# One PSUM pool for both phases of an attention-then-experts kernel, and another order of its first microseconds

## The chip, the cores and the metric

The kernel runs on one core of a Trainium2 chip. The core has five engines with queues of their own: TensorE (PE, with its weight loads PEld), VectorE (DVE), ScalarE (ACT), GpSimd (POOL) and SyncE (SP), which here only issues DMAs. DMAs issued from POOL and SP run on 16 DMA engines that all queues share. The metric is the time of one execution on the device, in microseconds (us); the median of several runs counts.

## What is computed

The reference is a gated attention unit without softmax, followed by a mixture of experts. Cut to what matters:

```python
scores = (1.0 / S) * np.matmul(z, z.transpose(0, 2, 1))    # z: 8 x 2816 x 64
attn = np.maximum(scores, 0.0) ** 2
x = (u * np.matmul(attn, v)).reshape(B * S, D)             # u, v: 8 x 2816 x 256
...
y_dense = np.maximum(x @ w1_dense, 0.0) @ w2_dense         # 256 -> 512 -> 256
expert_idx = np.argmax(x @ w_gate, axis=1)                 # 8 experts
for e in range(E):
    mask = expert_idx == e
    h = np.maximum(x[mask] @ w1[e], 0.0)
    y_moe[mask] = gate_w[mask, None] * (h @ w2[e])         # gate_w: softmax weight of the expert
out = y_dense + y_moe
```

Inputs and output are float32; the products on TensorE are bfloat16.

## The kernel before

**Phase one, attention.** There are 8 batches of 22 blocks of 128 rows (nK = 22, 176 blocks in all). Queries are taken in groups of 2 or 4 blocks, six groups to a batch. For a group, `scores` (line 390) multiplies z's turned blocks on PE into a pair of PSUM banks, and `relu` (line 412) offers two elementwise steps for each such tile: a scaled relu out of PSUM into a float32 buffer r (`first`, lines 420 and 422), and a square of r into the bfloat16 tile A (`second`, lines 433 and 435). The relu can run on ACT or DVE; the square on ACT or DVE, or, in the first two groups, on ACT or POOL. `av` (line 577) then multiplies A by v into an o tile in two passes over the keys (line 603), for two query blocks at a time, and `gate_x` (line 626) multiplies o by u on DVE (line 630) and issues a transposing DMA. Blocks of A that an earlier group has already as their mirror image are turned by DMA (line 487) and not computed again.

All of this is put in order while the program is built: `now` is the modelled time on PE, `free` that at which ACT, DVE and POOL come free, `offer`, `best` and `run` hand elementwise steps to whichever engine ends first by the model, and `need` takes the keys in the order in which A (`key_at`) and v (`v_at`, line 527) are expected. On the chip each engine runs its own instructions strictly in that order.

PSUM has eight banks. Phase one divides them into NS = 4 pairs, tags b0 to b3 of the pool ps, handed out by `take_pair` and given back by `give_pair`.

**The start.** The first batch's z comes in four parts (keys 0 to 3, 4 to 9, 10 to 15, 16 to 21), each loaded by SP, cast and doubled to bfloat16 by `cast_z0` (parts 0 and 2 on DVE, 1 on ACT, 3 on POOL), turned on PE (line 191) and copied out of PSUM by `turn_z0` (parts 0 and 2 on DVE, 1 and 3 on ACT). `scores` calls `turn_z0` as its keys ask for it, with four keys to spare: the first call, for keys 0 to 3, turns parts 0 and 1 ahead of its own matmuls. POOL issues v in four parts with `load_v`, two early and two after the constants: a select for the triangle ntri, four iotas, the cast of part 3 and the load of the gating weights wg stand between or behind them. `gate=True` puts a one-column memset on DVE in front of a load.

**Routing.** After 11 blocks `routing` computes gate logits (`logits`, line 651, which reads wg), picks the expert and the row (`route_a`, `route_pre`, which reads ntri, `route_b`), and one `scatter` per tick (line 749, on POOL) moves a block of rows to its expert's place in DRAM. A tick is a step of one block.

**Phase two, experts.** Each `slot` (line 1025) takes 256 rows of one expert: a transposed `fetch` on SP (line 924), the dense first layer and the expert's first layer (`up`, line 964: eight matmuls into an h_ps tile of two banks, line 973, and a relu on ACT, line 976), and two halves of 128 rows (`half`, line 991: `down` puts dense and expert result into one yy tile of one bank, line 982; ACT copies the dense part, line 999; DVE multiplies and adds, line 1000; POOL scatters the rows to the output, line 1002). On PE ups and halves alternate. The h tiles come from a pool psS with three buffers and the yy tiles from psY with two; both are opened after the pool of phase one is closed (lines 1192 to 1194). The last two routing groups use these pools too (`small`, line 645). A last part of the program runs only if the rows need more tiles than usual.

Of the kernel before, what the change touches and what calls it, by code (L numbers as in the profile page):

```python
# [8 lines left out]
F32 = mybir.dt.float32  # L9
# [3 lines left out]
ALU = mybir.AluOpType  # L13
AX = mybir.AxisListType
ET = mybir.EngineType
P = 128
# [3 lines left out]
def kernel(  # L20
# [12 lines left out]
    nc = tc.nc  # L33
    B, S, D = u.shape
# [43 lines left out]
    NS = 4  # L78
    attention = ExitStack()
    ps = attention.enter_context(tc.tile_pool(name="ps", bufs=1, space=bass.MemoryType.PSUM))  # L80
    late = {}
# [104 lines left out]
    def turn_z0(n):  # L186
# [19 lines left out]
        if n % 2:  # L206
            give_pair(z0_turned[n], x)

    load_v(0, 0, 4)
    cast_z0(0)  # L210
    cast_z0(1)
    load_v(0, 1, 4)
    nc.gpsimd.affine_select(out=ntri[:], in_=ntri[:], compare_op=ALU.is_ge,
                            fill=0.0, base=0, pattern=[[-1, P]],
                            channel_multiplier=1)
    ti = aw.tile([P, G, E], I32, name="ti", tag="xT", bufs=8)
# [6 lines left out]
    pj = const.tile([P, 1], I32, name="pj")  # L223
    nc.gpsimd.iota(pj[:], pattern=[[0, 1]], base=0, channel_multiplier=1)
    cast_z0(3)
    load_v(0, 2, 4, gate=False)
    load_v(0, 3, 4, gate=False)
    z0_left = list(range(len(parts0)))
    z0_cast = [0.0, 1.1, 0.0, 2.8]
    z0_turned = [0.0] * len(parts0)  # L230
    free.update(act=1.1, pool=4.2)

    nc.gpsimd.dma_start(out=wg[:], in_=moe_w_gate.rearrange("(c p) e -> p c e", p=P))
    sf = const.tile([P, N // T2], F32, name="sf")
# [4 lines left out]

    def small_constants():  # L240
        nc.vector.tensor_copy(desc8[:], ti[:])
# [148 lines left out]
    def scores(n, ks, x=None):  # L390
# [4 lines left out]
        c = w * P  # L395
        while n == 0 and z0_left and parts0[z0_left[0]][0] <= ks[-1] + 4:
            turn_z0(z0_left.pop(0))
# [11 lines left out]
        relu(n, ks, s, c, now[0] + 0.2, sx)  # L409
        run(now[0])  # L410

    def relu(n, ks, s, c, ready, sx):
# [37 lines left out]

        offer(ready, 1, {"act": (0.12 + c / 600, first), "dve": (0.1 + c / 480, first)}, half)

# [74 lines left out]
    def v_at(n, k):  # L527

        return 3.3 + 2.6 * (4 * k // nK) if n == 0 else 0.0

# [46 lines left out]
    def av(n, i, between):  # L577
# [9 lines left out]
        ox = take_pair()  # L587
        o = banks(ox, "o")
        for p in range(2):
            rest = list(range(nK))  # L590
# [54 lines left out]
    def small(q, name, shape):  # L645
        if q < nQ - 2:
            return banks(bank_of[q], name, shape)
        tag = "y" if q == nQ - 2 else "s"
        return late[tag].tile(list(shape), F32, name=name, tag=tag)

# [313 lines left out]
    def up(xT, ws):  # L964

        m = xT.shape[1]
        h_ps = late["s"].tile([P, 4, 2, P], F32, name="h_ps", tag="s")
        n = m // len(ws)
# [22 lines left out]
    def half(s, j):  # L991
# [3 lines left out]
        yd, ys = take("yd"), take("ys")  # L995
        y = late["y"].tile([P, 2, D], F32, name="yy", tag="y")
        down(y, 0, hd, lambda f: w2d[:, f, :], j)
# [191 lines left out]
    while jobs:  # L1189
        jobs.pop(0)[1]()  # L1190
        run(9e9)
    attention.close()
    late["s"] = pool("psS", 3, space=bass.MemoryType.PSUM)
    late["y"] = pool("psY", 2, space=bass.MemoryType.PSUM)
    for s in range(NT - MAYBE + 2):
# [47 lines left out]
```

## Time and profile before

| what | us |
|---|---|
| runs of the kernel before | 904.14, 905.04, 910.75 |
| median | 905.04 |
| the profiled execution | 909.34 |
| its span, first to last instruction | 907.6 |
| PE busy | 862.3 (95%) |
| ACT busy | 697.8 (77%) |
| DVE busy | 667.2 (74%) |
| POOL busy | 468.1 (52%) |
| first matmul of A with v (line 603) | starts at 10.1 |
| last one | starts at 550.1 |
| first h_ps matmul | starts at 552.0 |

The profile comes from one execution, and its span leaves out what lies before the first and after the last instruction. A row of the timeline gives the start, the length, the engine (a q behind it means its queue processor), the line and the operation, what is written from what, how many like instructions are merged in it, and in brackets how long the engine was idle before and what released it. Matmuls overlap one another in the array, so a row's mean duration is longer than the step from one to the next. The clock granted to TensorE was 0.998 over the span.

### The profile page before, as it was taken

The numbers are of one execution on the slowest core, as the hardware profiler recorded it, in microseconds if no ns is written. First come the engines' busy times: TensorE is split into PE (matmuls) and PEld (weight loads), VectorE is DVE, ScalarE is ACT, GpSimd is POOL, SyncE is SP. The second block draws the span as 40 slices with busy tenths as digits, with TensorE's granted clock in tenths as the row PEclk, the third lists the DMA queues.
The fourth block names the chain that finished last, engine by engine and source line by source line (L and its number), as shares of the span: only waits on it lengthen the run. The fifth ranks groups of instructions, "written<-read, shape, count | busy, mean of one in ns | idle before, by whom it ended". The sixth has DMA issues, their size and how long they took to land.

```text
span 907.6 us, 30096 instructions
## 1 busy us (share of the span) xinstructions
PE 862.3 (95%) x12178; PEld 754.2 (83%) x12178; DVE 667.2 (74%) x1268; ACT 697.8 (77%) x871; POOL 468.1 (52%) x510
## 2 busy tenths in 40 slices
PE   7999999999999999999999999988989898999996
PEld 5898798898898888889889877877878787888885
DVE  7998898898889889889889976456644444546554
ACT  8988798888889879879879964666666666776664
POOL 8202343343353444343334354777778777877454
PEclk9999999999999999999999999999999999999999
DMA  9999999999999999999998874645434453443332
GB/s 179 156 192 165 184 193 169 201 196 180 213 182 186 199 178 187 199 175 195 205 178 153 163 126 94 129 113 116 112 101 115 108 109 107 109 103 100 88 89 83
DMA packets 288238, 136.80 MB, mean 151 GB/s; under 512 B 258526, under 2 KB 265950, under 8 KB 287200
## 3 DMA queue, kind: packets, MB, share of 16 engines
q1 hardware_dynamic: 263552, 79.40, 52.5%
q0 software_dynamic: 24544, 55.44, 26.3%
q8 instruction: 96, 1.57, 0.7%
q14 instruction: 46, 0.38, 0.1%
HBM read 61.54 MB, written 37.03 MB: 109 GB/s over the span
## 4 chain that ended last, share of the span: by engine, by line
PE 70%; POOL 10%; issue 9%; DVE 4%; ACT 3%; DMA 2%; POOLq 0%; another core or an unknown queue 0%; DVEq 0%; SPq 0%; ACTq 0%
PE o L603 41%; PE yy L982 9%; PE h_ps L973 9%; PE s L405 9%; POOL out_dram L1002 7%; POOL zr L987 1%; DMA out_dram<-ring,ix 1%; ACT A L433 1%; ACT r L420 1%; DVE r L422 1%; PE lg L659 1%; POOL A L435 1%; DMA wall<-A 1%; DVE ring L1000 1%; ACT ring L999 1%
## 5 line engine op out<-in xcount | busy, mean ns | idle before, releaser
L603 PE MATMUL o<-vb,A 64*128 64x256 bf16 x7184 | 458.9, 269 | 3.1 <-POOL A L435 1.3
L603 PEld LDWEIGHTS <-A 64*128 64x128 bf16 x7184 | 378.8, 94 | 44.2 <-issue 3.3
L749 POOL DMA_INDIRECT xs<-pays,pi x176 | 191.9, 1090 | 283.0 <-DVE pi L747 232.1
L420 ACT ACTIVATE r<-s 128x1024 f32<-128x1024 f32 (+1 forms) x252 | 247.1, 1011 | 44.4 <-PE s L405 42.1
L976 ACT ACTIVATE ring<-h_ps 128x1024 bf16<-128x1024 f32 x180 | 184.6, 1027 | 96.1 <-PE h_ps L973 61.1
L433 ACT ACTIVATE A<-r 128x1024 bf16<-128x1024 f32 (+1 forms) x238 | 242.1, 1047 | 7.3 <-DMA wall<-A 4.6
L1000 DVE SCALAR_TENSOR_TENSOR ring<-yy,me,ring 128x256 f32<-128x256 f32 x179 | 85.6, 481 | 154.3 <-ACT ring L999 82.9
L435 DVE TENSOR_TENSOR A<-r 128x1024 bf16<-128x1024 f32 x151 | 182.9, 1221 | 4.0 <-ACT r L420 3.0
L422 DVE TENSOR_SCALAR r<-s 128x1024 f32<-128x1024 f32 (+1 forms) x145 | 175.0, 1214 | 8.7 <-PE s L405 6.0
L1002 POOL DMA_INDIRECT out_dram<-ring,me x140 | 147.1, 1051 | 66.2 <-DVE ring L1000 31.2
L982 PEld LDWEIGHTS <-ring 128*128 128x128 bf16 x1432 | 138.9, 98 | 44.6 <-issue 28.9
L405 PE MATMUL s<-zT 64*128 64x512 bf16 (+1 forms) x874 | 145.1, 355 | 1.8 <-ACT zT L199 0.6
L982 PE MATMUL yy<-w2d,ring 128*128 128x256 bf16 x716 | 107.3, 272 | 22.8 <-DVE ring L1000 20.2
L982 PE MATMUL yy<-ring 128*128 128x256 bf16 x716 | 107.6, 273 | 0.3 <-issue 0.3
L973 PE MATMUL h_ps<-ring 128*128 128x256 bf16 (+1 forms) x872 | 94.6, 254 | 1.2
L973 PE MATMUL h_ps<-ring,w1d 128*128 128x256 bf16 x720 | 93.1, 272 | 2.3 <-DVE pays L630 1.6
L999 ACT COPY ring<-yy 128x256 f32<-128x256 f32 x179 | 67.7, 378 | 29.2 <-PE yy L982 18.1
L960 DVE COPY ring<-wall 128x2048 bf16 x109 | 81.8, 765 | 10.2 <-issue 6.2
L630 DVE TENSOR_TENSOR pays<-o,ut 128x512 bf16<-128x512 f32 x88 | 60.2, 685 | 30.6 <-PE o L603 29.0
L973 PEld LDWEIGHTS <-ring 128*128 128x128 bf16 x872 | 73.0, 98 | 11.7 <-DVE ring L960 2.7
L973 PEld LDWEIGHTS <-w1d 128*128 128x128 bf16 x720 | 69.9, 98 | 11.0 <-issue 3.0
L405 PEld LDWEIGHTS <-zT 64*128 64x128 bf16 x874 | 54.2, 94 | 17.5 <-issue 6.7
(122 smaller groups left out, 426.6 us busy)
## 6 DMA issues: line engine op xcount, KB each, us to landing
ut<-in_u_dram SPq DMA_DIRECT2D x88, 256.0 KB
vb<-in_v_dram POOLq DMA_DIRECT2D x7, 1408.0 KB
wall<-in_moe_w_dram POOLq DMA_DIRECT2D x16, 256.0 KB
xs<-pays,pi POOLq DMA_INDIRECT x176
zr<-in_z_dram POOLq DMA_DIRECT2D x7, 352.0 KB
out_dram<-ring,me POOLq DMA_INDIRECT x140
ring<-xs SPq DMA_TRANSPOSE x114
xT<-pays SPq DMA_TRANSPOSE x88
```

Of the source, the lines that this page charges most:

```text
L405: nc.tensor.matmul(out=s[:, h, y * c:(y + 1) * c], lhsT=zT[r, k + h, :], rhs=zT[r, i0:i0 + w, :], start=True, stop=True)
L420: nc.scalar.activation(r[:, :, :c], s[:, :, :c], AF.Relu, scale=1.0 / S)
L422: nc.vector.tensor_scalar(out=r[:, :, :c], in0=s[:, :, :c], scalar1=1.0 / S, scalar2=0.0, op0=ALU.mult, op1=ALU.max)
L433: nc.scalar.activation(a, r, AF.Square)
L435: (nc.gpsimd if eng == "pool" else nc.vector).tensor_mul(a, r, r)
L603: nc.tensor.matmul(out=o[:, j, 0:D], lhsT=block(n, k, i + j - i0)[r], rhs=v_of[b][r, k, :], start=(p == 0 and x == 0), stop=(p == 1 and x ...
L749: ins = nc.gpsimd.indirect_dma_start(out=xs, out_offset=bass.IndirectOffsetOnAxis(ap=pi[:], axis=0), in_=pays[:, g % (2 * G), 0:ROW].bitca ...
L973: nc.tensor.matmul(out=h_ps[:, f, hs, :], lhsT=w1(c, f), rhs=xT[:, hs, c, :], start=(c == 0), stop=(c == 1))
L976: nc.scalar.activation(h[:, :, 0:m * P], h_ps[:, :, 0:m, :].rearrange("p f h t -> p f (h t)"), AF.Relu)
L982: nc.tensor.matmul(out=y[:, k, :], lhsT=h[:, f, j * P:(j + 1) * P], rhs=w2(f), start=(f == 0), stop=(f == 3))
L1000: nc.vector.scalar_tensor_tensor(out=ys, in0=y[:, 1, :], scalar=me[:, j, 0:1], in1=yd, op0=ALU.mult, op1=ALU.add)
L1002: ins = nc.gpsimd.indirect_dma_start(out=out, out_offset=bass.IndirectOffsetOnAxis(ap=ids[j], axis=0), in_=ys, in_offset=None, bounds_chec ...
```

## The change

The diff does five things. The pool ps stays open for the whole kernel: the pairs that phase one leaves become, for phase two, one pair for both yy tiles (a bank each, two views of one tile) and three pairs for h, with the pair of the last o at the end of that row; `next_h` and `next_y` take them in rotation. The first call of `scores` turns only part 0 ahead of its matmuls, and part 1 with the second call. The relu of the first score tile can only go to DVE, and the model runs 0.4 us further there, so that it is put in before the next part is turned. On POOL the iotas stand ahead of v, the four parts of v are issued in one go with a gate on the first alone, and the cast of part 3 follows; the expected times of v (`v_at`) and of POOL's start are moved to match. The load of wg and the select for ntri go into `small_constants`, which is called at tick 2.

```diff
-    attention = ExitStack()
-    ps = attention.enter_context(tc.tile_pool(name="ps", bufs=1, space=bass.MemoryType.PSUM))
+    ps = pool("ps", 1, space=bass.MemoryType.PSUM)
+    last_o = []
...
-    load_v(0, 0, 4)
-    cast_z0(0)
-    cast_z0(1)
-    load_v(0, 1, 4)
-    nc.gpsimd.affine_select(out=ntri[:], in_=ntri[:], compare_op=ALU.is_ge,
...
     nc.gpsimd.iota(pj[:], pattern=[[0, 1]], base=0, channel_multiplier=1)
+    for h in range(4):
+        load_v(0, h, 4, gate=h == 0)
+    cast_z0(0)
+    cast_z0(1)
     cast_z0(3)
-    load_v(0, 2, 4, gate=False)
-    load_v(0, 3, 4, gate=False)
...
-    z0_cast = [0.0, 1.1, 0.0, 2.8]
+    z0_cast = [0.0, 1.1, 0.0, 2.4]
...
-    free.update(act=1.1, pool=4.2)
-
-    nc.gpsimd.dma_start(out=wg[:], in_=moe_w_gate.rearrange("(c p) e -> p c e", p=P))
+    free.update(act=1.1, pool=2.4)
...
     def small_constants():
+        nc.gpsimd.dma_start(out=wg[:], in_=moe_w_gate.rearrange("(c p) e -> p c e", p=P))
+        nc.gpsimd.affine_select(out=ntri[:], in_=ntri[:], compare_op=ALU.is_ge,
...
-        while n == 0 and z0_left and parts0[z0_left[0]][0] <= ks[-1] + 4:
+        while n == 0 and z0_left and parts0[z0_left[0]][0] <= ks[-1] + (4 if ks[0] else 1):
...
-        run(now[0])
+        run(now[0] + (0.4 if n + ks[0] == 0 else 0.0))
...
+        ways = {"act": (0.12 + c / 600, first), "dve": (0.1 + c / 480, first)}
+        if n + ks[0] == 0:
+            del ways["act"]
+        offer(ready, 1, ways, half)
...
-        return 3.3 + 2.6 * (4 * k // nK) if n == 0 else 0.0
+        return 2.8 + 2.5 * (4 * k // nK) if n == 0 else 0.0
...
+        if q == nQ - 1:
+            return next_h(name, shape)
+        a, b = shape[1:]
+        return next_y()[:, 0:a * b].rearrange("p (a b) -> p a b", b=b)
+
+    def next_h(name, shape):
+        late["h"].append(late["h"].pop(0))
+        return banks(late["h"][-1], name, shape)
+
+    def next_y():
+        late["y"].append(late["y"].pop(0))
+        return late["y"][-1]
...
-        h_ps = late["s"].tile([P, 4, 2, P], F32, name="h_ps", tag="s")
+        h_ps = next_h("h_ps", (P, 4, 2, P))
...
-        y = late["y"].tile([P, 2, D], F32, name="yy", tag="y")
+        y = next_y().rearrange("p (k d) -> p k d", d=D)
...
-    attention.close()
-    late["s"] = pool("psS", 3, space=bass.MemoryType.PSUM)
-    late["y"] = pool("psY", 2, space=bass.MemoryType.PSUM)
+    other = [x for _, x in pairs if x not in last_o]
+    assert len(other) == NS - 1
+    yy = banks(other.pop(0), "yy")
+    late["y"] = [yy[:, x, :] for x in range(2)]
+    late["h"] = other + last_o
```

More of the change, by code (lines that the diff above doesn't have):

```diff
@@ L207, in turn_z0 @@
             give_pair(z0_turned[n], x)
-    load_v(0, 0, 4)
-    cast_z0(0)
-    cast_z0(1)
-    load_v(0, 1, 4)
-    nc.gpsimd.affine_select(out=ntri[:], in_=ntri[:], compare_op=ALU.is_ge,
-                            fill=0.0, base=0, pattern=[[-1, P]],
-                            channel_multiplier=1)
     ti = aw.tile([P, G, E], I32, name="ti", tag="xT", bufs=8)
@@ L240, in small_constants @@
     def small_constants():
+        nc.gpsimd.dma_start(out=wg[:], in_=moe_w_gate.rearrange("(c p) e -> p c e", p=P))
+        nc.gpsimd.affine_select(out=ntri[:], in_=ntri[:], compare_op=ALU.is_ge,
+                                fill=0.0, base=0, pattern=[[-1, P]],
+                                channel_multiplier=1)
         nc.vector.tensor_copy(desc8[:], ti[:])
@@ L449, in half @@
             offer(t + 0.15, 4, ways, done)
-        offer(ready, 1, {"act": (0.12 + c / 600, first), "dve": (0.1 + c / 480, first)}, half)
+        ways = {"act": (0.12 + c / 600, first), "dve": (0.1 + c / 480, first)}
+        if n + ks[0] == 0:
+            del ways["act"]
+        offer(ready, 1, ways, half)
     def can_turn(n, m):
@@ L588, in av @@
         o = banks(ox, "o")
+        last_o[:] = [ox]
         for p in range(2):
@@ L647, in small @@
             return banks(bank_of[q], name, shape)
-        tag = "y" if q == nQ - 2 else "s"
-        return late[tag].tile(list(shape), F32, name=name, tag=tag)
+        if q == nQ - 1:
[8 more added lines that the diff above has]
+        return late["y"][-1]
     def logits(q):
```

## The prediction

> **What bounds the kernel now.** I read the page's busy shares and its chain of waits first, then the stages, and then the two places the change touches: the first 25 us and the seam between the phases. The chain, by engine and by line:
>
> ```profile
> PE 70%; POOL 10%; issue 9%; DVE 4%; ACT 3%; DMA 2%; POOLq 0%; another core or an unknown queue 0%; DVEq 0%; SPq 0%; ACTq 0%
> PE o L603 41%; PE yy L982 9%; PE h_ps L973 9%; PE s L405 9%; POOL out_dram L1002 7%; POOL zr L987 1%; DMA out_dram<-ring,ix 1%; ACT A L433 1%; ACT r L420 1%; DVE r L422 1%; PE lg L659 1%; POOL A L435 1%; DMA wall<-A 1%; DVE ring L1000 1%; ACT ring L999 1%
> ```
>
> TensorE carries the chain. The stages say where it doesn't (stretch, its length, then busy us of PE, PEld, DVE, ACT, POOL, the clock, the DMA share and GB/s):
>
> ```profile
> core 0 of [0], span 907.6 us
> core 0: us, PE busy (x) PEld busy (x) DVE busy (x) ACT busy (x) POOL busy (x), PEclk, DMA share, GB/s
> 0.00:10.00 10.00, 6.99 (x68) 4.77 (x68) 6.64 (x12) 6.18 (x7) 7.84 (x20) 1.00 0.80 162
> 5.00:6.00 1.00, 1.00 (x14) 0.59 (x13) 0.08 (x1) 0.48 (x1) 1.00 (x5) 1.00 0.75 110
> 10.00:25.00 15.00, 12.63 (x178) 8.79 (x180) 12.39 (x16) 14.26 (x16) 12.71 (x9) 1.00 1.16 187
> 25.00:50.00 25.00, 24.45 (x400) 21.18 (x398) 24.83 (x34) 23.71 (x26) 4.28 (x8) 1.00 0.92 162
> 400.00:500.00 100.00, 99.72 (x1707) 88.22 (x1708) 88.16 (x160) 85.88 (x95) 39.39 (x39) 1.00 1.04 181
> 600.00:640.00 40.00, 35.72 (x320) 30.85 (x318) 20.96 (x41) 23.37 (x37) 31.44 (x38) 1.00 0.55 119
> 760.00:820.00 60.00, 57.56 (x526) 51.14 (x525) 28.63 (x50) 40.98 (x65) 46.39 (x54) 1.00 0.44 106
> ```
>
> From 400 to 500 us PE idles 0.28 us in 100. What can be won in the attention phase lies in the first 25 us, where PE idles 3.0 and 2.4 us. Right after that DVE and ACT are full (24.83 and 23.71 of 25), so early gains must also be gains of the elementwise engines. In the second phase PE idles 4.3 us of 40, then 2.4 of 60; no edit touches its steady pattern, only its first instant and its buffers.
>
> **The start, part by part.** GpSimd's queue in order of time (start, length):
>
> ```profile
> 3.01 1.33 POOL L130 DMA_DIRECT2D vb<-in_v_dram  x2 [1.47 <-DVE vb L129]
> 4.35 0.31 POOL L213 TENSOR_SCALAR_AFFINE_SELECT ntri<-ntri 128x128 bf16<-128x128 bf16 x1
> 4.60 0.67 POOL L218 IOTA tok<- 128x176 int32 x1
> 5.23 0.12 POOL L220 IOTA te<- 128x8 int32 x1
> 5.32 0.19 POOL L222 IOTA it<- 128x88 int32 x1
> 5.48 0.12 POOL L224 IOTA pj<- 128x1 int32 x1
> 5.56 0.81 POOL L180 CAST zn<-z 128x768 bf16<-128x768 f32 x1
> 6.33 1.07 POOL L130 DMA_DIRECT2D vb<-in_v_dram  x2
> 7.39 0.73 POOL L233 DMA_DIRECT2D wg<-in_moe_w_gate_dram  x1
> 8.12 1.93 POOL L435 TENSOR_TENSOR A<-r 128x1024 bf16<-128x1024 f32 x1
> ```
>
> The four iotas (0.67 + 0.12 + 0.19 + 0.12 = 1.10 us) move into the 1.47 us in which the queue waits for the gate of the first v load: free, with 0.37 to spare. The select and the wg load (0.31 + 0.73 = 1.04) go to tick 2, behind the first squares; the next user of both is the first routing, many ticks later, and POOL is busy 4.28 us of 25 in that stretch, which hides them; without that cover they would cost 1.04 us of POOL. The queue becomes four v issues, 3.01 + 1.33 + 1.07 = 5.41, then the cast of z's last part to 6.22. So POOL reaches its first square at about 6.2 instead of 8.12, if a score tile has been through its first relu by then. The second v load also loses its gate, a memset on DVE that is already passed: nothing.
>
> VectorE around the same time:
>
> ```profile
> 4.13 0.42 DVE L197 COPY zT<-zp 128x512 bf16<-128x512 bf16 x1 [0.69 <-PE zp L191]
> 4.47 0.60 DVE L184 CAST zn<-z 128x768 bf16<-128x768 f32 x1
> 6.29 0.56 DVE L197 COPY zT<-zp 128x768 bf16<-128x768 bf16 x1 [1.21 <-PE zp L191]
> 6.81 1.23 DVE L422 TENSOR_SCALAR r<-s 128x1024 f32<-128x1024 f32 x1
> ```
>
> The first part of z is turned by 4.55. In the new order the scores of keys 0 to 3 stand next on PE, so they are there by about 5.0, when DVE ends its cast (5.07). The relu takes 1.23; the idle time ahead of the copy at 6.29 is 1.21. It fits almost exactly, ends at 6.30 and delays that copy by 0.01. Behind it queue only that copy and DVE's next relu. What the new order delays is the turning of the second part on PE, by the four small matmuls set in front of it, 0.2 to 0.4 us, and so ACT's copy of it and the second score tile. I take 0.2, which the next steps hide, since ACT is spared its first relu (about 1 us; the row stands below).
>
> So r stands at 6.30 and POOL's first square can start at about 6.4: 1.7 us earlier. What does PE gain? Its two stalls after the first keys:
>
> ```profile
> 14.68 0.55 PE L603 MATMUL o<-vb,A 64*128 64x256 bf16 x4 [1.08 <-DMA vb<-in_v_dram]
> ```
>
> ```profile
> 22.96 0.79 PE L603 MATMUL o<-vb,A 64*128 64x256 bf16 x8 [0.85 <-POOL A L435]
> ```
>
> The first is the landing of v. The last two v parts are issued about 2.1 us earlier (6.33 to 4.3), but the DMA share is 1.16 in the stretch they land in, so the load is limited by bandwidth; what is won is the hole of 5 to 6 us (share 0.75, so 0.25) and some priority over the transposes that come after 11 us. The bounds are 0 and 2.1; I take 0.4, nearest to the hole. The second stall ends on a square of POOL, whose chain starts 1.7 earlier: all of the 0.85 can go, and the next limit is then DVE and ACT. Together 0.4 + 0.85 = 1.25. Against it the elementwise limit: the early start wins one relu on DVE and one square on POOL, which is one score tile. Their prices:
>
> ```profile
> L435 DVE TENSOR_TENSOR A<-r 128x1024 bf16<-128x1024 f32 x151 | 182.9, 1221 | 4.0 <-ACT r L420 3.0
> L422 DVE TENSOR_SCALAR r<-s 128x1024 f32<-128x1024 f32 (+1 forms) x145 | 175.0, 1214 | 8.7 <-PE s L405 6.0 <-POOL A L435 1.5 <-ACT A L433 0.6
> ```
>
> ```profile
> L420 ACT ACTIVATE r<-s 128x1024 f32<-128x1024 f32 (+1 forms) x252 | 247.1, 1011 | 44.4 <-PE s L405 42.1 <-DVE A L435 0.7 <-POOL A L435 0.6
> L433 ACT ACTIVATE A<-r 128x1024 bf16<-128x1024 f32 (+1 forms) x238 | 242.1, 1047 | 7.3 <-DMA wall<-A 4.6 <-DVE r L422 1.0 <-issue 0.4
> ```
>
> A tile costs ACT 1.01 + 1.05 = 2.06 and DVE 1.21 + 1.22 = 2.43; together they make one per 1 / (1/2.06 + 1/2.43) = 1.12 us. So one tile ahead is 1.1 us, the smaller of the two. **Start: 1.1 us won**, bounds 0 (v sets everything) and 1.9 (0.4 + 0.85 plus the rest of the 1.7).
>
> A rule speaks against part of it. The two v issues that lay beside VectorE's SBUF cast took 1.33 together, the two beside its copy out of PSUM 1.07: a difference of 0.13 each. The Trainium skill (SBUF — State Buffer, section Who interferes with whom) says that a VectorE copy or cast in its two-port mode locks GpSimd out of the shared SBUF port for the whole instruction, and that descriptor generation suffers. By that rule the new third issue, which falls on the cast of 4.47 to 5.07, could stand for up to its 0.60, and the start would win 0.5 instead of 1.1; the trace supports a tenth of a microsecond, not the full lock.
>
> **The seam.** Before, phase two has its own PSUM pools, opened when the old one closes:
>
> ```profile
> 551.98 1.03 PE L973 MATMUL h_ps<-ring,w1d 128*128 128x256 bf16 x8 [1.64 <-DVE pays L630]
> ```
>
> PE waits 1.64 us for VectorE's last gating product, though that product reads only the last o. With one pool the first h tile takes a pair that was freed earlier, so PE goes straight on. Next late is slot 1's transposed fetch:
>
> ```profile
> 550.05 1.21 SPq L924 DMA_TRANSPOSE ring<-xs  x1
> ```
>
> PE would want it after two ups and the small logits, 551.98 - 1.64 + 0.87 + 0.87 + 0.2 = 552.3 (0.87 per up is in the chain row further down; 0.2 for the small logits is an estimate). The queue's issue alone lasts to 551.26 and its landing isn't shown; before, PE used it here and didn't wait:
>
> ```profile
> 553.92 1.03 PE L973 MATMUL h_ps<-ring,w1d 128*128 128x256 bf16 x8
> ```
>
> So the landing lies between 551.26 and 553.92. I put it at 552.7, near the middle, which costs 0.4 of the 1.64. **Seam: 1.2 us won**, bounds 0.4 and 1.64; the first output scatter moves with it, so the POOL part of the later chain does too.
>
> The rest of the pool edit changes names only: three h buffers of two banks and two y buffers of one bank, taken in the same rotation.
>
> **Sum.** 1.1 + 1.2 = 2.3 us. The profiled execution took 909.34 us (span 907.6, so 1.7 outside it), 4.3 above the median of the three runs, 905.04. I predict 907.0 for the like execution and 905.04 - 2.3 = 902.7 us as the median.
>
> **Rivals.** *Seam or start gives nothing* (0.20): the fetch or v's landing takes over; then 904, with only one of the terms left. *The new plan drifts* (0.12): the order after the start is made from modelled times, so other relus land on other engines over 500 us. PE's busy time from 40 to 540 us bounds it:
>
> ```profile
> sum 500.00, PE 495.99; mean PE 19.84
> ```
>
> That is 4.0 us of idle time, so a drift is worth up to 4 us either way: 902.7 + 4.0 = 906.7, or 898.7. *More than counted* (0.06): all bounds at once, 1.9 + 1.64 plus some drift, 900 to 901.
>
> *Slower: the two y buffers become one* (0.07). They are now halves of one tile that lives through the whole phase. If waits are made per tile and not per bank, each half must wait for the readers of the half before. Rows for the price, the relu that may stand ahead on ACT, ACT's copy, DVE's product, and the up that lies between two halves on PE:
>
> ```profile
> 555.00 1.02 ACT L976 ACTIVATE ring<-h_ps 128x1024 bf16<-128x1024 f32 x1
> 555.91 0.37 ACT L999 COPY ring<-yy 128x256 f32<-128x256 f32 x1
> ```
>
> ```profile
> 556.31 0.48 DVE L1000 SCALAR_TENSOR_TENSOR ring<-yy,me,ring 128x256 f32<-128x256 f32 x1
> ```
>
> ```profile
> 570.11 0.87 PE h_ps L973 x8
> ```
>
> Copy and product with three handovers (0.04 each, an estimate) are 0.97, against 0.87 of cover: 0.1 us of stall per half, and up to 1.1 where a relu stands ahead of the copy. Times 179 halves that is 18 to 200 us; with half a relu, 0.6 x 179 = 107, about 1010 us. It decides as soon as one half waits for the other. Against it: the SBUF rings of this kernel are cut from single tiles as well, and there PE reads one slice of ring while ACT writes another without a wait (the relu at 555.00 lies beside this product):
>
> ```profile
> 555.23 0.60 PE L982 MATMUL yy<-ring 128*128 128x256 bf16 x4
> ```
> That is SBUF, so the trace doesn't settle it for PSUM. The Trainium skill (PSUM — Partial Sum Buffer, section PSUM bank collisions raise a hardware error) asks for semaphores by bank, and the halves lie in two banks; by that rule nothing waits and this rival is worth nothing.
>
> **How the numbers follow.** The forecast as worked out has 0.55; with the rivals above that is 1.00. One per cent, 9 us, is about what a measurement of this kernel can tell from no change. Only the y rival passes it on the slow side; with 0.01 for a drift that large, slower is 0.08. Faster by 9 us would need more than all idle time named here: 0.02. Within 1%: 0.90. The range reaches from the bounds with some drift, 899.5, up to the drift against the change, 906.7, and a little of the spread of runs, 907.5; it leaves out the y rival and little else.
>
> **What would show it.** The start: a POOL square beginning near 6.4, DVE's first relu near 5.1, the v stall on PE shorter or earlier, the 0.85 us stall on POOL's square gone. The seam: no wait of the first h_ps for pays, 0 to 0.4 us for a fetch instead. The y halves: the wait of yy for DVE's ring product as before; if it grows by tens of microseconds, the y rival is true. I'm wrong if PE's idle time in the middle of phase one moves by more than 2 us, or if the first output scatter doesn't come earlier.

## The result: slower by four per cent, and the profile after

| what | before | after |
|---|---|---|
| median of 6 runs each, us | 906.32 | 943.45 |
| lowest to highest | 904.14 to 911.93 | 940.36 to 946.36 |
| the profiled execution | 909.34 | 944.55 |
| its span | 907.6 | 942.8 |
| last matmul of A with v starts | 550.1 | 552.1 |
| from there to the end of the span | 357.5 | 390.7 |

The ratio of the medians is 1.040, with a 95% interval of 1.036 to 1.044. The forecast was 902.7 us, 899.5 to 907.5. In the kernel after, line numbers have moved: o is L605, h_ps L985, its relu L988, yy L994, ACT's copy of yy L1011, VectorE's product L1012 and the fetch L936.

The last two rows of the table place the loss: phase one ends 2 us later, and phase two is 33 us longer. The 2 us say little: nine traces of kernels with the phase one of the kernel before, it among them, end it between 547.7 and 552.3 us. The stages of the kernel after, with the columns of the prediction's stages:

```profile
10.00:25.00 15.00, 11.71 (x145) 7.67 (x145) 11.67 (x16) 12.40 (x15) 10.41 (x8) 0.89 1.13 205
25.00:50.00 25.00, 24.41 (x392) 20.96 (x394) 24.86 (x33) 23.57 (x25) 4.31 (x8) 1.00 0.83 131
400.00:500.00 100.00, 99.72 (x1711) 88.38 (x1709) 88.06 (x159) 86.25 (x96) 39.23 (x40) 1.00 1.00 181
600.00:640.00 40.00, 35.08 (x297) 28.75 (x296) 20.18 (x46) 25.21 (x38) 28.97 (x35) 1.00 0.41 103
760.00:820.00 60.00, 54.20 (x457) 44.37 (x456) 24.16 (x46) 39.54 (x57) 43.19 (x49) 1.00 0.40 100
```

The middle of phase one is as it was: PE is busy 99.72 of 100 us in both. From 760 to 820 us PE, DVE, ACT and POOL all do less in the same time (from 600 to 640 us all but ACT). The matmul count says it best: 457 instead of 526 from 760 to 820 us. No engine there has become the bound; everything waits. For what, PE's waits tell (what waited, for what, us in all, times, longest). After:

```profile
PE yy L994 <- DVE ring L1012: 28.6, 80, 1.3
PE yy L994 <- issue: 3.5, 19, 0.5
PE o L605 <- DMA vb<-in_v_dram: 1.9, 1, 1.9
PE h_ps L985 <- DMA ring<-xs: 1.8, 2, 1.1
```

Before:

```profile
PE yy L982 <- DVE ring L1000: 20.2, 22, 2.4
PE yy L982 <- issue: 2.3, 4, 0.9
```

The sum has grown by 8.4 us only, and whoever stops there misses the loss. The number of places went from 22 to 80, and the single wait became shorter: a few long holds have become a steady pattern. The weight loads carry more of it (busy us and mean ns, then idle time before them), since they wait beside a blocked matmul:

```profile
L994 PEld LDWEIGHTS <-ring 128*128 128x128 bf16 x1432 | 138.8, 97 | 84.8 <-issue 70.0
```

Before, this row (L982) has 44.6 us of idle time. The pattern itself stands in the timeline of the kernel after, two halves from the middle of phase two:

```profile
781.54 1.02 ACT L988 ACTIVATE ring<-h_ps 128x1024 bf16<-128x1024 f32 x1 [0.50 <-PE h_ps L985]
781.66 0.60 PE L994 MATMUL yy<-w2d,ring 128*128 128x256 bf16 x4 [0.16 <-DVE ring L1012]
781.66 0.75 PEld L994 LDWEIGHTS <-ring 128*128 128x128 bf16 x7 [0.34 <-issue]
...
782.10 0.60 PE L994 MATMUL yy<-ring 128*128 128x256 bf16 x4
...
782.53 1.04 PE L985 MATMUL h_ps<-ring,w1d 128*128 128x256 bf16 x8
...
782.73 0.37 ACT L1011 COPY ring<-yy 128x256 f32<-128x256 f32 x1 [0.17 <-PE yy L994]
...
783.14 0.48 DVE L1012 SCALAR_TENSOR_TENSOR ring<-yy,me,ring 128x256 f32<-128x256 f32 x1 [0.58 <-ACT ring L1011]
...
783.67 0.60 PE L994 MATMUL yy<-w2d,ring 128*128 128x256 bf16 x4
```

Read it as one chain; call the time from the start of one half to the start of the next a turn. The eight matmuls of a half take 781.66 to 782.70. ACT copies from 782.73, VectorE multiplies from 783.14 to 783.62, and the next half starts at 783.67, 0.05 behind the product that read the other half of the same PSUM tile. A turn takes 2.01 us: 1.04 of matmuls and 0.97 of copy, product and handovers. PE's own work in a turn is about 1.75: 0.87 for the half's eight matmuls, from the first start to the start of what follows, and as much for the up between. The rest is PE standing still, in pieces too small to look like a stall.

The mean turn over phase two comes from the first and last start of the yy rows (duration min, median, max in ns, then the two starts). Before:

```profile
L982 PE MATMUL yy<-w2d,ring x716: 269/272/273, 554.8 to 898.7; 128*128 128x256 bf16 x179
```

After:

```profile
L994 PE MATMUL yy<-w2d,ring x716: 269/271/273, 556.5 to 936.4; 128*128 128x256 bf16 x179
```

179 halves have 178 steps: 343.9 / 178 = 1.93 us before, 379.9 / 178 = 2.13 after. The difference, 0.20 us x 178 = 36 us, is the whole of the loss; the span grew by 35.2 us, since the first yy comes 1.7 later and the stretch behind the last one is 2.5 shorter.

### The profile page after: what moved, and what is told of

The parts are those of the page before. It is cut to its first block, busy times and chain, and to the rows that moved or that the text cites. A ratio compares the mean times of both kernels' runs of the same rounds, so it can differ in the third digit from the quotient of the medians.

```text
span 942.8 us, 30096 instructions
## 1 busy us (share of the span) xinstructions
PE 883.6 (94%) x12178; PEld 755.6 (80%) x12178; DVE 665.8 (71%) x1269; ACT 717.1 (76%) x871; POOL 470.2 (50%) x508
## 5 line engine op out<-in xcount | busy, mean ns | idle before, releaser
L605 PE MATMUL o<-vb,A 64*128 64x256 bf16 x7184 | 460.6, 269 | 4.2 <-DMA vb<-in_v_dram 1.9
L605 PEld LDWEIGHTS <-A 64*128 64x128 bf16 x7184 | 379.5, 94 | 46.0 <-issue 5.2
L761 POOL DMA_INDIRECT xs<-pays,pi x176 | 197.3, 1121 | 282.1 <-DVE pi L759 231.6
L988 ACT ACTIVATE ring<-h_ps 128x1024 bf16<-128x1024 f32 x180 | 183.3, 1019 | 93.5 <-PE h_ps L985 83.0
L1012 DVE SCALAR_TENSOR_TENSOR ring<-yy,me,ring 128x256 f32<-128x256 f32 x179 | 86.4, 483 | 187.6 <-ACT ring L1011 75.6
L994 PEld LDWEIGHTS <-ring 128*128 128x128 bf16 x1432 | 138.8, 97 | 84.8 <-issue 70.0
L1014 POOL DMA_INDIRECT out_dram<-ring,me x140 | 154.6, 1104 | 86.5 <-DVE ring L1012 56.8
L420 DVE TENSOR_SCALAR r<-s 128x1024 f32<-128x1024 f32 x147 | 178.0, 1218 | 10.4 <-PE s L403 9.7
L994 PE MATMUL yy<-w2d,ring 128*128 128x256 bf16 x716 | 106.9, 271 | 40.3 <-DVE ring L1012 28.6
L994 PE MATMUL yy<-ring 128*128 128x256 bf16 x716 | 107.4, 273 | 0.0
L1011 ACT COPY ring<-yy 128x256 f32<-128x256 f32 x179 | 66.6, 372 | 48.9 <-PE yy L994 29.9
L985 PE MATMUL h_ps<-ring,w1d 128*128 128x256 bf16 x720 | 92.9, 272 | 1.8 <-DMA ring<-xs 1.8
L985 PE MATMUL h_ps<-ring 128*128 128x256 bf16 (+1 forms) x872 | 93.2, 253 | 0.0
L972 DVE COPY ring<-wall 128x2048 bf16 x109 | 76.2, 714 | 17.6 <-issue 9.2
L985 PEld LDWEIGHTS <-ring 128*128 128x128 bf16 x872 | 73.9, 98 | 6.8
L985 PEld LDWEIGHTS <-w1d 128*128 128x128 bf16 x720 | 69.8, 98 | 10.2 <-DMA ring<-xs 2.0
```

The lines of the kernel that those rows point to most:

```text
L420: nc.vector.tensor_scalar(out=r[:, :, :c], in0=s[:, :, :c], scalar1=1.0 / S, scalar2=0.0, op0=ALU.mult, op1=ALU.max)
L605: nc.tensor.matmul(out=o[:, j, 0:D], lhsT=block(n, k, i + j - i0)[r], rhs=v_of[b][r, k, :], start=(p == 0 and x == 0), stop=(p == 1 and x ...
L761: ins = nc.gpsimd.indirect_dma_start(out=xs, out_offset=bass.IndirectOffsetOnAxis(ap=pi[:], axis=0), in_=pays[:, g % (2 * G), 0:ROW].bitca ...
L985: nc.tensor.matmul(out=h_ps[:, f, hs, :], lhsT=w1(c, f), rhs=xT[:, hs, c, :], start=(c == 0), stop=(c == 1))
L988: nc.scalar.activation(h[:, :, 0:m * P], h_ps[:, :, 0:m, :].rearrange("p f h t -> p f (h t)"), AF.Relu)
L994: nc.tensor.matmul(out=y[:, k, :], lhsT=h[:, f, j * P:(j + 1) * P], rhs=w2(f), start=(f == 0), stop=(f == 3))
```

## The experiments

The kernels were run in six batches, each on one chip beside runs of the kernel before. That kernel's median was 909.4, 915.4, 874.6, 917.1, 877.4 and 907.8 us in them, so ratios are taken within a batch. The first theory was the slow rival of the prediction: the two y halves have become one tile of PSUM, the memory into which PE writes its sums, and every half waits for the readers of the half before. Its own rival was that the new order of the start or the seam disturbs the later plan.

**The shared tile alone, and everything but the shared tile** (batch 1). `one_y_alone` is the kernel before with this one edit:

```diff
...
-    late["y"] = pool("psY", 2, space=bass.MemoryType.PSUM)
+    late["y"] = pool("psY", 1, space=bass.MemoryType.PSUM)
+    yy = late["y"].tile([P, 2, 4 * P], F32, name="yy")
+    late["yy"] = [yy[:, x, :] for x in range(2)]
```

> The kernel before with one edit: both yy buffers are halves of one PSUM tile that lives through phase two, a bank each, taken in rotation; pools, start and seam stay. Theory (each half of yy waits for VectorE's product of the half before, since the wait is made for the tile): the second phase takes some 33 us more, 906 + 33 = 939 us, and the yy matmuls wait for VectorE in about 80 places instead of 22. Rival (waits are made by bank, so the halves stay independent, and the 35 us come from the seam, the h rotation or the start): 906 us, within 2.

`after_two_y` is the kernel after, with pair 2 in a pool of its own that is closed at the end of phase one and makes room for two y tiles:

```diff
...
-    yy = banks(other.pop(0), "yy")
-    late["y"] = [yy[:, x, :] for x in range(2)]
+    other.remove(YP)
+    ypair.close()
+    late["y"] = pool("psY", 2, space=bass.MemoryType.PSUM)
```

> The changed kernel with one edit: the pair of banks that held the yy tile becomes a pool of its own with two yy tiles, a fresh one for each half; everything else of the change stays. Theory (the shared yy tile costs the 33 us): 943 - 33 = 910 us, the wait of yy for VectorE back to about 22 places. Rival (one pool for the h tiles, the seam or the start costs it): stays at 935 us or more.

Measured: `one_y_alone` 939.32 us, ratio 1.034 (1.029 to 1.039); `after_two_y` 908.52, ratio 1.000 (0.997 to 1.003). The waits follow. `one_y_alone`:

```profile
PE yy L988 <- DVE ring L1006: 25.6, 79, 1.4
```

`after_two_y`:

```profile
PE yy L996 <- DVE ring L1014: 18.4, 21, 1.9
```

One edit alone brings 79 places, and its removal alone goes back to 21. The cause is settled by this pair. All other parts of the change together gave nothing that could be measured; the interval of `after_two_y` reaches some 2.4 us down, so a gain as small as the forecast's 2.3 us isn't ruled out by the times alone.

**One buffer** (batch 2). Does the tile with two banks act like a single buffer? `y_one_buffer` is the kernel before with `pool("psY", 1, ...)`, the tiles taken as before.

> The kernel before with a single yy buffer (one pool buffer instead of two), nothing else. Theory (two views of one tile work as one buffer): the same second phase as with the shared tile, 939 us, the yy matmuls waiting for VectorE in about 80 places. Rival (the shared tile is more than the loss of a buffer, or less, since the halves still overlap in part): differs from 939 by more than 5 us.

Measured: 945.88 us, ratio 1.033 (1.027 to 1.039), where the shared tile had 1.034 in batch 1. Its waits:

```profile
PE yy L982 <- DVE ring L1000: 28.6, 84, 1.4
```

So the second bank of the shared tile bought nothing.

**Start alone and seam alone** (batch 1). `start_alone` has every edit of the start and no other; `seam_alone` has the one pool of the change, but with separate y tiles.

> The kernel before with the start edits alone: GpSimd's order, the scores of the first keys ahead of the turning of the next, first relu on VectorE; PSUM pools as before. Theory (TensorE reaches v's last part sooner, idles 1.9 us for it, its granted clock falls to one half for about 3.4 us, and the first phase ends 2 us later): 906 + 2 = 908 us. Rival (the predicted gain of one score tile, 1.1 us, and the 2 us of the changed kernel came from one slow landing of v): 905 us.

> The kernel before with the one PSUM pool, but with two yy tiles in a pool of their own; start as before. Theory (the first h no longer waits for VectorE's last gating product, 1.6 us, but the transposed fetches of the second and third tile then end last, so nothing of it is kept): 906 us, within 1. Rival (the predicted seam gain): 905 us or less, with the first output scatter 1.2 us earlier after the last matmul of phase one.

Measured: 908.99 us, ratio 0.9995 (0.997 to 1.002), and 906.88, ratio 0.998 (0.996 to 1.001). Neither gives a gain that stands out of its interval. In the trace of `start_alone` PE waits 1.3 us for v, and the granted clock, which its theory saw fall, stays full there. Starts of the nth matmul of A with v, from the traces:

| n | before | start_alone | after |
|---|---|---|---|
| 1 | 10.1 | 8.6 | 8.3 |
| 41 | 15.3 | 15.2 | 16.1 |
| 88 | 18.9 | 19.4 | 20.8 |
| 352 | 39.9 | 40.3 | 41.7 |

The 1.5 us of lead of the first matmul is used up by the 41st. What the kernel after loses beyond `start_alone` goes with its clock, which falls to a half for 3.41 us at 14.37 us (see below). In all the traces taken, six falls lie between 14 and 16 us. In five of these the 352nd matmul comes at 41.5 to 42.5 (two, `more_slots` and `seam_fetch`, have the old start), in the sixth, with matmuls added, at 43.1. In nine traces without a fall before 40 us it comes at 39.8 to 40.6, in a tenth, `v_in_one_go`, at 42.2.

**What eats the start?** `start_no_v3` (batch 2) is `start_alone` without the load of the last quarter of the first batch's v, which stays zero.

```diff
...
-    for h in range(4):
+    v_of[0] = zpool.tile([P, nK, D], BF, name="vb")
+    nc.gpsimd.memset(v_of[0][:, 3 * nK // 4:, :], 0.0)
+    for h in range(3):
```

> The start edits alone, and the last quarter of the first batch's v isn't loaded but set to zero by GpSimd, so the output leaves it out. Theory (the landing of v ends last at the start, so what the elementwise engines win is lost there): TensorE's 41st matmul with v, at 15.2 us with the load, comes before 14 us, and the first phase ends at least 1 us sooner than the start edits alone. Rival (ScalarE, VectorE and GpSimd limit the start): it still comes near 15 us and phase one ends as late.

One execution: 914.65 us beside 915.38. PE no longer waits for v. The 41st matmul started at 14.3, 0.9 sooner than in `start_alone`, the 88th at 19.1 (19.4) and the 176th at 27.2 (27.3). So the landing of v holds the 41st matmul and no longer the 176th, and the theory that it sets the whole start falls. Its other sign, an earlier end of phase one, can't be read: that came at 556.4 instead of 553.2, behind a wait of PE of 2.70 us up to 34.67 us and a fall of the clock at 34.52. Past the first keys the elementwise engines are the likely limit, as the prediction's second bound had it: from 20 to 25 us of `start_alone` DVE is busy 4.87 us, ACT 4.88 and PE 4.22. No run isolates it.

`scores_first` and `v_in_one_go` (batch 3) are the two halves of the start: the order of scores and turning with the first relu on VectorE, and GpSimd's order with v in one go.

> The kernel before with the PE order alone: scores of the first keys ahead of the turning of the next, first relu on VectorE; GpSimd's queue as before. Theory (v's landing sets the start): TensorE's first matmul with v comes up to 1.5 us sooner than 10.1, its 41st no sooner than 15, its 352nd at 40 within 0.5 unless the clock falls. Rival (the elementwise head start counts): the 352nd at 39 or sooner.

> The kernel before with GpSimd's order alone: constants first, v issued in one go, gating weights and select later; scores and first relu as before. Theory (the load is limited by bandwidth): TensorE still waits for v's last quarter until 14.4 to 15, the 352nd matmul with v at 40 within 0.5. Rival (earlier issue brings v sooner, as the forecast's 0.4 us had it, or more): the wait ends by 14.2 and the 352nd comes before 39.5.

One execution each: 875.07 and 876.76 us beside 874.57. Neither half shows a gain, and the traces agree: in `scores_first` the first matmul of A with v starts at 8.5, but PE then waits 2.6 us for v, the clock falls at 15.17 and the 352nd comes at 42.5; in `v_in_one_go` PE doesn't wait for v, and the 352nd comes at 42.2 all the same.

`two_y_warm` (batch 2) was meant for the clock. In the kernel after, the granted clock falls to a half at 14.37 us, within the wait for v that ends at 14.91. The stretches (the clock is the third figure from the end):

```profile
14.00:15.00 1.00, 0.09 (x2) 0.09 (x3) 0.00 (x0) 0.73 (x1) 0.18 (x1) 0.68 0.38 55
15.00:16.00 1.00, 1.00 (x10) 0.64 (x11) 0.15 (x1) 0.00 (x0) 0.00 (x0) 0.50 1.13 348
16.00:17.00 1.00, 1.00 (x11) 0.73 (x9) 1.00 (x1) 0.00 (x0) 0.00 (x0) 0.50 1.06 342
17.00:18.00 1.00, 1.00 (x10) 0.56 (x8) 0.31 (x3) 0.67 (x1) 0.85 (x1) 0.61 1.21 299
```

It is `after_two_y` with 24 small matmuls ahead of v's last quarter, whose sums nobody reads:

```diff
...
+                if n == 0 and i == i0 and p == 0 and 4 * k // nK == 3 and not kept:
+                    kept.append(x)
+                    for _ in range(24):
+                        nc.tensor.matmul(out=o[:, 0, 2 * P:3 * P], lhsT=ones[:], rhs=ones[:],
+                                         start=False, stop=False, skip_group_check=True)
```

> The changed kernel with two yy tiles, and 24 small matmuls into an unused part of the o tile, whose sums nobody reads, in front of the first matmul that needs the last quarter of v: TensorE is busy for some 1.3 us of its wait. Theory (the wait of about 2 us lets the granted clock fall to one half for 3.4 us): no row of clock one half between 10 and 20 us, and TensorE's 352nd matmul with v at about 40.5 us instead of 42.1. Rival (the clock falls for another reason, or its fall costs nothing): half clock again, or the 352nd matmul at 42 us all the same.

Measured: 920.76 us, ratio 1.005 (1.002 to 1.009). Its trace shows that it tested nothing:

```profile
14.37 0.40 PE L615 MATMUL o<-vb,A 64*128 64x256 bf16 x2 [1.62 <-DMA vb<-in_v_dram]
14.54 0.65 PE L406 MATMUL s<-zT 64*128 64x512 bf16 x2
15.12 2.72 PE L610 MATMUL o<-ones 128*128 128x128 bf16 x24
```

PE waits for an earlier quarter than the one I had taken. The 24 matmuls stand behind that wait, at 15.12, when the clock had fallen already (at 14.27). They cost 2.7 us and kept nothing warm. Whether work inside the wait would hold the clock wasn't tried.

**What eats the seam?** In `seam_alone` PE no longer waits for VectorE's gating product, and waits for the fetches:

```profile
PE h_ps L988 <- DMA ring<-xs: 2.2, 2, 1.3
```

`seam_fetch` (batch 2) issues the second and third fetch a tick sooner.

```diff
-        at(nB - 3 + s, lambda s=s: first_fetch(s))
+        at(nB - 3 + max(s - 1, 0), lambda s=s: first_fetch(s))
```

> The seam edit alone with two yy tiles, and the transposed fetch of the second tile issued one tick sooner, right behind the first one's, and that of the third a tick sooner. Theory (at the seam the fetches end last): the waits of h_ps for a fetch in the first tiles, 2.2 us in the seam kernel, fall under 1 us and the first yy matmuls come 1 to 2 us sooner after the last matmul of phase one; 905 us. Rival (another engine, GpSimd's scatters or VectorE's routing, holds the first tiles): the waits go and nothing comes sooner; 907 us.

Measured: 917.4 us, ratio 1.003 (1.000 to 1.007). PE still waited 1.9 us for fetches. The first yy matmul came 3.0 us after the start of the last o (4.5 in `seam_alone`, 4.7 before), the 41st 15.2 (15.4, 15.1), the 81st 25.2 (24.3, 24.2): nothing is kept.

**Is another division of the banks better?** `two_h_four_y` (batch 3): two h tiles and four y tiles in the kernel before.

> The kernel before with PSUM of phase two shared out the other way: two h buffers of two banks and four yy buffers of one bank, instead of three and two. Theory (a yy buffer less costs 33 us because each half then waits for its predecessor's readers; two already cover that): at least 906 us, slower by the loss of an h buffer. Rival (yy buffers still limit the second phase): under 900 us.

Measured: 875.5 us, ratio 1.000 (0.997 to 1.003). No gain. But in this batch phase two took some 316 us in all three kernels traced, where the kernel before had 349 in its first profile. The stages of `scores_first`:

```profile
640.00:700.00 60.00, 60.00 (x552) 53.76 (x551) 31.55 (x65) 44.36 (x69) 49.28 (x60) 1.00 0.57 120
700.00:760.00 60.00, 60.00 (x553) 53.78 (x551) 28.66 (x58) 44.32 (x70) 50.98 (x64) 1.00 0.55 121
```

PE is busy without a gap, so this batch can't tell what more y tiles would do where PE has gaps; that stays open. On the other batches something else holds the halves as well, and the question is how the shared tile's cost adds to it: as a fixed amount, or as a floor of 2.01 us under each turn.

**A floor or a fixed amount?** `before_look` and `one_y_again` (batch 4) are the kernel before and `one_y_alone` once more.

> The kernel before, unchanged, for a profile on the chip of this call. First theory (the shared tile adds its loop of 2.01 us per half in place of whatever held the halves before): if this chip is one where phase two is bound by PE alone, phase two takes about 316 us and yy hardly waits for VectorE; if it is like the first chip, about 355 us with some 20 us of waits of yy for VectorE and some more for weights. Rival (the long phase two belongs to the changed programs, not to the chip): phase two takes 347 to 356 us on every chip.

> The kernel before with the two y halves as views of one PSUM tile, on the chip of this call. First theory (each half waits for the VectorE product of the half before, so a half takes at least 1.04 + 0.97 = 2.01 us): the cost is 179 halves times 2.01 less what a half takes in the kernel before here: up to 45 us (ratio 1.05) if phase two took 316 us there, about 30 us (1.034) if it took 355. Rival (a fixed extra per half, whatever else holds the halves): 31 us (1.034) in both cases.

Measured: 917.97 us, and 945.73 with a ratio of 1.032 (1.027 to 1.037). Phase two of the kernel before took 356 us up to its last yy here, so this batch couldn't tell the two apart. `more_slots` and `more_slots_one_y` (batch 5) tried to take away the suspected other hold, the SBUF slots of finished halves that output scatters still read:

```diff
+        four = zpool.tile([P, nK, D], BF, name="vb")[:].rearrange("p k d -> p (k d)")
+        ring["ys"] += cut(four, 0, 11, 2 * D)
```

> The kernel before with 19 instead of 8 SBUF slots for the finished half (eleven more cut from a v tile that phase two has no use for), y tiles separate. Theory (VectorE's product waits for the output scatter that still reads its slot; this is the part of its idle time that the profile puts to issue, 48 us in 42 places in the kernel before): that idle time falls by most of its size, yy waits less for VectorE, and phase two takes 316 to 335 us instead of 355 (ratio 0.96 to 0.98) on a chip where the kernel before needs 905 us or more. Rival (the slots are not what holds the product; it waits for ACT's copy or for the fetched gate values): same time within 0.5 per cent.

> The same eleven slots, with the two y halves as views of one PSUM tile. If the shared tile sets a floor under each half (2.01 us): about the time of the shared tile alone, ratio 1.02 to 1.034, even if the separate tiles gain 3 per cent by the slots, so the difference to more_slots grows to 35 to 48 us. If it adds a fixed 31 us: 31 us above more_slots whatever that takes.

Measured: 875.08 us, ratio 0.998 (0.995 to 1.001), and 928.84, ratio 1.059 (1.054 to 1.064). The batch was one in which the kernel before needs 877.4 us, so it says nothing on the slots, but it tells floor and fixed amount apart: the two differ by 54 us, well above 31 and above the 35 to 48 expected of the floor. The yy rows of `more_slots`:

```profile
L984 PE MATMUL yy<-w2d,ring x716: 272/273/273, 554.2 to 866.6; 128*128 128x256 bf16 x179
```

`more_slots_one_y`:

```profile
L990 PE MATMUL yy<-w2d,ring x716: 269/271/273, 552.0 to 920.6; 128*128 128x256 bf16 x179
```

A turn takes 312.4 / 178 = 1.755 us with separate tiles, which is PE's own 1.75, and 368.6 / 178 = 2.07 with the shared one. A fixed amount (31 us / 178 = 0.17) would have given 1.93. So the shared tile acts as a floor, some 0.06 above the 2.01 of the turn read above: the cost is 54 us where nothing else holds the halves, and 29 to 37 where the turn took 1.92 to 1.97 anyway and 2.12 to 2.14 with the shared tile.

`more_slots_again` (batch 6) repeats `more_slots`.

> The kernel before with 19 slots for the finished half, once more, since the last call fell on a chip where phase two of the kernel before takes about 316 us and nothing holds VectorE's product. If this chip is of the other kind (kernel before 905 us or more): theory of the slots, ratio 0.96 to 0.98 and the idle time of VectorE's product put to issue falls from 48 us; rival, ratio 0.995 to 1.005. On the quick kind the run tells nothing on this and gives 0.995 to 1.003.

Measured: 910.82 us beside 907.82, ratio 1.003 (1.000 to 1.006). VectorE's product still idles:

```profile
DVE ring L1002 <- issue: 21.3, 13, 3.3
DVE vb L1002 <- issue: 20.6, 15, 3.0
```

41.9 us in 28 places, where the kernel before has 48.2 in 42. The slots aren't what holds it, and that theory falls. No version tried here beats the kernel before.

## Why the prediction was wrong

**The step that failed** is one sentence: "The rest of the pool edit changes names only: three h buffers of two banks and two y buffers of one bank, taken in the same rotation." Its paragraph on what bounds the kernel says the same of phase two: "no edit touches its steady pattern, only its first instant and its buffers." The rotation was the same, but not what waits on what. Two tiles of a pool are waited for one by one; two views of one tile were waited for together (`after_two_y`, 21 places; `one_y_alone`, 79). The prediction had that as a rival and gave it 0.07.

**The two arguments against the rival.** The first was that SBUF rings cut from one tile show no such wait. The rows were right, but they showed a PE read beside an ACT write of an SBUF tile, and the rival was on a PSUM tile that PE writes while VectorE still reads it: another memory and another pair of accesses. The prediction said that SBUF doesn't settle it for PSUM and went on as if it did. Why the rings escape the wait wasn't tried. The second argument was the page PSUM — Partial Sum Buffer (section PSUM bank collisions raise a hardware error) of the Trainium skill: guard by bank, so halves in two banks need no wait. That says which guard is needed, not which one a program has. Here the measurement decides: the guard covered the whole tile, at 1.034.

**The price of the rival.** Its loop was right: copy, product and handovers were put at 0.97, and the timeline has 0.97. The stall of 0.1 per half was too small, since the cover was set against 0.87 of up alone. A half's matmuls end 1.04 after the first starts, while the next matmul may start after 0.87; that 0.17 also lies on the loop. 2.01 less 1.75 is 0.26 a turn, 47 us in 179. The further bound, a relu ahead of ACT's copy (up to 1.1 per half, 200 us), didn't come: in the timeline above the relu of 781.54 to 782.56 stands in time in which ACT would wait for the half's matmuls anyway. The rival's middle figure, 107 us, was three times what it cost. In the profiled pair the turn before was 1.93 and not 1.75, so a bare floor of 2.01 would cost 0.08 x 178 = 14 us. It cost 36, since the floor is 2.07 on the mean of all halves and some of the other holds, 0.06 a turn, come on top. The sign that the prediction set for this rival, a wait of yy for VectorE that grows by tens of microseconds, didn't show either: the wait grew by 8.4 us, and the idle time of the weight loads by 40.2.

**The start: 1.1 us forecast, nothing kept.** VectorE's first relu came nearly as worked out:

```profile
5.28 1.22 DVE L420 TENSOR_SCALAR r<-s 128x1024 f32<-128x1024 f32 x1
6.41 0.55 DVE L197 COPY zT<-zp 128x768 bf16<-128x768 bf16 x1
```

It was forecast for 5.07 to 6.30, and the copy came at 6.41 instead of 6.30. POOL's first square was forecast for 6.4. It came at 8.33:

```profile
5.48 0.84 POOL L180 CAST zn<-z 128x768 bf16<-128x768 f32 x1
6.25 0.71 POOL L235 DMA_DIRECT2D wg<-in_moe_w_gate_dram  x1
8.33 1.89 POOL L433 TENSOR_TENSOR A<-r 128x1024 bf16<-128x1024 f32 x1 [1.37 <-DVE r L420]
```

POOL was free at 6.3, 0.1 later than forecast, but the plan gave the first square to ACT:

```profile
6.53 1.06 ACT L431 ACTIVATE A<-r 128x1024 bf16<-128x1024 f32 x1
```

I had assumed the engine of that square instead of reading it from the rule that hands squares to whichever engine ends first. And wg's load ran ahead of the squares, not behind them; its cover, POOL's wait, hid it as said. VectorE's lock on GpSimd's descriptors, weighed in the prediction, didn't show: the four v issues took 3.01 to 5.48, 2.47 instead of 1.33 + 1.07, though VectorE's cast ran beside them from 4.80 to 5.36. The stall of 0.85 on POOL's square is gone, but one of 0.55 on ACT's square stands at 25.03. The wait of PE for v was not shorter but 1.92 instead of 1.08, for v landed no sooner (PE went on at 14.91 instead of 14.68), and in the profiled execution the clock fell to a half within that wait. (The issue of v's last two parts was to come 2.1 earlier; the prediction's own figures, 6.33 and 4.3, give 2.0.) The interval of `start_alone` would hold a gain of 1.1 us too; that nothing is kept is read from the starts of the 41st and later matmuls.

**The seam: 1.2 us forecast, a ratio of 0.998 measured, whose interval holds 1.2 us and nothing alike.** The first h_ps started right behind o, and the fetches took the place of the wait as foreseen, at 1.8 us in two places instead of 0.4 in one:

```profile
552.35 1.05 PE L985 MATMUL h_ps<-ring,w1d 128*128 128x256 bf16 x8
...
552.87 1.21 SPq L936 DMA_TRANSPOSE ring<-xs  x1
...
555.57 1.05 PE L985 MATMUL h_ps<-ring,w1d 128*128 128x256 bf16 x8 [1.12 <-DMA ring<-xs]
...
559.40 1.05 PE L985 MATMUL h_ps<-ring,w1d 128*128 128x256 bf16 x8 [0.68 <-DMA ring<-xs]
```

The term was mis-sized, but not by the landing: from the issue of slot 1's fetch to its use the forecast had 2.65 us (550.05 to 552.7), and it took 2.70 (552.87 to 555.57). The prediction left the issue where it stood before, at the start of the last o (550.05, 550.07). It came 0.73 us behind that start (552.87, 552.14), so PE waited 1.12 instead of 0.4; what held the issue stays open. And only slot 1's fetch was weighed: slot 2's cost 0.68 more. The lower bound of 0.4 was also wrong by the prediction's own figures: a landing at 553.92, against PE's need at 552.3, takes 1.6 of the 1.64 and leaves nothing. The first h_ps started 1.9 us behind the start of the last o before (551.98, 550.1) and 0.2 now. The first output scatter is 6.6 us behind that start instead of 7.0, and the ninth yy matmul, the first of the next half, 8.3 instead of 7.4 (8.2 in `seam_alone`, where the y tiles are separate): what the seam won was gone by then.

## What to carry to other kernels

When buffers are merged into one tile, ask what the waits are attached to: here two banks were two buffers only as two tiles. Before a rival is dismissed by an analogy, check that the analogy has the same memory and the same pair of accesses; an edit of two lines that leaves the arithmetic alone can cost more than all the gains it was bundled with. And compare the number of waits as well as their sum: many equal short waits, one per turn, are a loop, and its length read from the timeline gives the cost.

## What the runs showed of the hardware that was not expected

The same program has two levels, some 40 us apart, and the level goes with the batch and not with the chip: batches 4 and 5 are both recorded on chip 7, with 917.1 and 877.4 us for the kernel before. Nearly all of it lies in phase two. On the high level ACT idles ahead of its copies of yy; in `more_slots_again`:

```profile
L1001 ACT COPY ring<-yy 128x256 f32<-128x256 f32 x179 | 67.7, 379 | 33.9 <-PE h_ps L975 20.8 <-PE yy L984 11.4 <-issue 1.3
```

On the low level this idle time is gone from the same kernel, in `more_slots`:

```profile
L1001 ACT COPY ring<-yy 128x256 f32<-128x256 f32 x179 | 65.8, 368 | 1.5 <-PE yy L984 1.5
```

What sets the level stays open. The second finding is the clock: it fell to a half within a wait of PE of 1.92 us, for 3.41 us, and such stretches of 3.41 us turned up at other places of other runs (663 us in `seam_alone`, 34.5 in `start_no_v3`). The Trainium skill (TensorE: Matmul & The Clock Gate, section Part 1: The HAM clock gate) gives a window of about 3.4 us that runs freely and doesn't start with the kernel; the length agrees. A single long wait is not what these falls have in common. In the 3.41 us ahead of the fall PE was busy 1.62 us in the kernel after, 1.00 in `seam_alone` and 0.86 in `start_no_v3`, and 0.86 to 1.99 ahead of all seventeen falls that these traces have before the end of PE's work. No limit can be read from that: in `more_slots` PE was busy 1.48 us from 554.69 to 558.10, and the clock stayed full.
